# A long convolution with a routed expert layer: the filter stage on single-bank PSUM tensors, with one two-sign copy a bank and products of ones between its groups

## The chip, the cores and the metric

The kernel runs on one core of a Trainium2 chip. The metric is device time in microseconds (us) for one launch. The engines are TensorE (PE; PEld is its weight load), VectorE (DVE), ScalarE (ACT), GpSimd (POOL) and SyncE (SP), which here only issues DMAs.

## What is computed

Inputs `x` and `v` are 4 x 12608 x 128, in float32. A filter is made by a small network over position embeddings, damped by a window, and convolved along the sequence; then 128 rows of each batch pass through an expert layer.

```
h_mlp  = maximum(pos_emb @ w1, 0) @ w2            # 12608x64 @ 64x64, @ 64x128
h_filt = h_mlp * exp(-0.01 * pos)
u = x * v
y = irfft(rfft(u, 2S) * rfft(h_filt, 2S))[:S]     # per batch and channel
x = x * y
scores = x @ w_gate                               # per batch: top 128 rows
x[top] += sigmoid(scores[top]) * (relu(x[top] @ w1e) @ w2e)
```

## The kernel before

The transforms are products with tables of cosines and sines. The sequence is laid out as a 91 x 254 grid. One program does the following in order.

**The filter** runs once, before anything else can finish. It has three stages.

- `h_hid` (L293): position embeddings times `w1`, in eight groups of 16 products (L331; the two halves `h` use different rows of the array). A product in float32 is two passes in the trace, so there are 254 passes for 127 products. A group's output is a two-bank PSUM tensor `c`, three of which rotate. The ReLU with the window goes to `big` (view `hw`) by DVE (L342), or for the second half of odd groups by ACT in eight small instructions (L339). DVE (L346) and POOL (L344) write a second copy with signs. Twenty products of a 128 x 128 bf16 tile of ones (L321) run ahead of the groups.
- `h_spec` (L348), first loop: 256 products of 92 columns (L354, 512 passes), 16 to each of 16 two-bank tensors. ACT alone copies each one to `th` in SBUF (L355), with the frequency outermost in the destination, so that consecutive elements land 512 bytes apart. In this text this loop is the spec loop.
- `h_spec`, second loop: 23 steps `i`. `second(i)` does eight products (L366) into bank `a` number `i % 2`, ACT copies half of it (L369), and DVE forms sum and difference (L372, two instructions). `final(i)` does eight products (L382) into a two-bank tensor: for each half `h` a bank with both signs `s`. ACT copies sign 0 of a bank (L392) and DVE sign 1 (L390) into `big` (view `sp_all`), 364 bytes apart from element to element. `second` runs two steps ahead.

**The main loop** has 128 steps `t` of four channels. `f_s1` (L410) and `dft` (L287) are forward transforms into the banks `a` and into `c1` or `c0` in turn; ACT copies out (L412, L290). DVE combines (`f_v` L419, `f_u` L416), multiplies by the filter (`f_m`, L424 and L425) and adds (`f_y`, L430 and L431). POOL forms `sd` (L437, L438). Three steps later `f_i` (L282) transforms back into `c2`. The first `f_s1` stands ahead of the last `final`. `stage_u` (POOL, L268) multiplies `x` by `v`. The selection of rows and the expert layer run in the gaps of the steps.

The order on each engine is the order in which the code issues. Waits come from tensors: an instruction waits for earlier users of the same PSUM tensor or the same piece of SBUF.

Of the kernel before, what the change touches and what calls it, by code (L numbers as in the profile page):

```python
# [10 lines left out]
F32 = mybir.dt.float32  # L11
AF = mybir.ActivationFunctionType
ALU = mybir.AluOpType
# [5 lines left out]
NQ = 64  # L19
# [160 lines left out]
def hyena_moe(ctx, tc, xg, x2, pos, bw, ww, wg, mw1, mw2, fo, fc, c1, gx, cf, ci, wm, tk, out):  # L180
# [26 lines left out]
    bank2 = [pp.tile([128, 1024], F32, tag=f"c{k}", name=f"c{k}") for k in range(3)]  # L207

    def ps1(k, shape, name):
        return view((*bank1, *bank2[::2])[k], 0, shape)  # L210

    def ps2(k, shape, name):
        return view(bank2[k], 0, shape)
# [70 lines left out]
    def dft(t, te, pq):  # L284
        for w in (1, 0):
            for a in range(0, 128, 32):
                nc.tensor.matmul(pq[w][a:a + 32], lhsT=cf_sb[:, 2 * w + a // NQ, a % NQ:a % NQ + 32],  # L287
                                 rhs=te[:, a // NQ], start=True, stop=True)
        qs = buf("qs", t, [128, HC])
        nc.scalar.copy(out=qs, in_=pq[1])  # L290
        return qs

    def h_hid():  # L293
        pt = view(arena, POS0, [128, PJ, N1])
        wl = view(arena, FILT + 381, [128, FO])
        nc.sync.dma_start(wl, bw)

        def load(k):
            nc.sync.dma_start(pt[:, PC * k:PC * (k + 1)], pos[:, PC * k:PC * (k + 1)])

        for k in range(PJ // PC):
            load(k)
            if k == 1:
                nc.sync.dma_start(wm_sb, wm)
        nc.sync.dma_start(fc_sb, fc)
        nc.sync.dma_start(fo_sb, fo)
        nc.sync.dma_start(ww_sb, ww)
        nc.sync.dma_start(c1_sb, c1)
        nc.sync.dma_start(cf_sb, cf)
        nc.sync.dma_start(ci_sb, ci)  # L310
        nc.sync.dma_start(gx_sb, gx)
        nc.sync.dma_start(wgb, wg.partition_broadcast(128))
        nc.sync.dma_start(tk_sb, tk)
        for k in range(NV):
            load_u(k)
            stage_u(k)

        def warm(n, w):
            wp = ps2(2, [w.shape[0], w.shape[1]], "warm")
            for _ in range(n):  # L320
                nc.tensor.matmul(wp[:w.shape[1]], lhsT=w, rhs=w, start=True, stop=True)  # L321

        warm(20, onesb)
        for k in range(PJ // PC):
            a, z = PC * k, PC * (k + 1)
            ps = ps2(k % 3, [N1, 2, PC, FO], f"hid_{k}")
            for j in range(a, z):
                for h in range(2):
                    if h * PJ + j < N3:
                        r = slice(h * FO, (h + 1) * FO)  # L330
                        nc.tensor.matmul(ps[:, h, j - a], lhsT=pt[r, j], rhs=wl[r], start=True, stop=True)  # L331
            for h in range(2):
                j0, j1 = h * PJ + a, min(h * PJ + z, N3)
                o = hw[:, :, :, j0:j1]
                pv = ps[:, h, :j1 - j0].rearrange("p j d -> p d j")
                wb = wm_sb[:N1, :, j0:j1].unsqueeze(2).to_broadcast([N1, 3, FO, j1 - j0])
                if h and k % 2:
                    for i in range(j1 - j0):
                        nc.scalar.activation(out=o[:, 0, :, i], in_=ps[:, h, i], func=AF.Relu,  # L339
                                             scale=wm_sb[:N1, 0, j0 + i:j0 + i + 1])  # L340
                else:
                    nc.vector.scalar_tensor_tensor(out=o[:, 0], in0=pv, scalar=0.0, in1=wb[:, 0], op0=ALU.max, op1=ALU.mult)  # L342
                if h:
                    nc.gpsimd.tensor_tensor(out=o[:, 1], in0=o[:, 0], in1=wb[:, 1], op=ALU.mult)  # L344
                else:
                    nc.vector.scalar_tensor_tensor(out=o[:, 1], in0=pv, scalar=0.0, in1=wb[:, 2], op0=ALU.max, op1=ALU.mult)  # L346

    def h_spec():  # L348
        for k in range(16):
            e, f = divmod(8 * k, FO)  # L350
            ps = ps2(k % 3, [128, 2, 512], f"ht_{k}")[:, :, :4 * N4].rearrange("p b (f k) -> p b f k", f=4)
            for i in range(8):
                for p in (slice(0, NQ), slice(NQ, N3)):
                    nc.tensor.matmul(ps[p, i // 4, i % 4], lhsT=hw[:, e, f + i, p], rhs=fc_sb, start=True, stop=True)  # L354
            nc.scalar.copy(out=th[:, :, e, f:f + 8].rearrange("p k (b f) -> p b f k", f=4), in_=ps[:N3])  # L355
        for k in range(NV, NU):
            load_u(k)
        stage_u(NV)
        hs = {}

        def second(i):
            ps = ps1(i % 2, [128, 2, 2, 2 * NQ], f"hq_{i}")
            for e in range(2):
                for c in (1, 0):
                    for h in range(2):
                        nc.tensor.matmul(ps[h * FO:(h + 1) * FO, c, e], lhsT=th[:, c * KH + i + KH // 2 * h, e],  # L366
                                         rhs=fo_sb[:N3, e, 1 - c:3 - c].rearrange("p a r -> p (a r)"), start=True, stop=True)
# [3 lines left out]
            for s, op in enumerate((ALU.add, ALU.subtract)):  # L371
                nc.vector.tensor_tensor(out=hs[i][:, s].rearrange("p w e r -> p e w r"),  # L372
                                        in0=ps[:, 0].rearrange("p e (w r) -> p e w r", w=2), in1=sb, op=op)

        def final(i):
            hb = hs.pop(i)
            ps = ps2(i % 3, [128, 2, 2, 2, D], f"hf_{i}")
            for s in range(2):
                for w in range(2):
                    for h in range(2):  # L380
                        r = slice(h * FO, (h + 1) * FO)
                        nc.tensor.matmul(ps[:, h, s, w], lhsT=hb[r, s, w].rearrange("p e r -> p (e r)"), rhs=ww_sb[r],  # L382
                                         start=True, stop=True)
# [12 lines left out]
        second(1)  # L396
        for i in range(n):
            if i == n - 1:
                te[0] = f_s1(0)
            final(i)  # L400
            if i + 2 < n:
                second(i + 2)

    def f_s1(t):
        u = buf("x", t, [NP, 4, N3])
# [660 lines left out]
        else:  # L1066
            picked.append((b, ix, xe))

    for t in bank2[2:] + bank1 + bank2[:2]:
        nc.vector.memset(t, 0.0)  # L1070
    te, uv, ys, sd, ph = {}, {}, {}, {}, {}
    h_hid()
    h_spec()
    ex = None
    bg = Background(iter(()))
    NT = B * NG
    for t in range(NT + LAG):
# [4 lines left out]
        if t < NT:  # L1082
# [4 lines left out]
            qs = dft(t, te.pop(t), (uv[t][:, 0], uv[t][:, 1]))  # L1087
            bg.hook("p", 1)
            bg.hook("n", 1)
            if t + 1 < NT:  # L1090
                te[t + 1] = f_s1(t + 1)
            spare[0] = None
            bg.hook("w", 1)
            load_u(t + NU)
            if t < NG:
                nc.sync.dma_start(hd[:, t], slots[:, t])
            for k in EARLY[t - 4:t - 3] if t > 3 else ():
                nc.scalar.activation(out=view(arena, XP[k], [128, 8 * D]), in_=one.to_broadcast([128, 8 * D]), func=AF.Copy,
                                     scale=0.0)
# [99 lines left out]
```

## Time and profile before

| | |
|---|---|
| median of 3 runs | 873.3 us (871.49 to 873.38) |
| profiled execution | 867.63 us |
| its span in the trace | 865.9 us |
| mean granted TensorE clock | 0.966 of 2.4 GHz |
| PE / PEld busy | 826.7 us (95%) / 697.9 us (81%) |
| DVE / ACT / POOL busy | 706.0 (82%) / 630.2 (73%) / 657.2 us (76%) |

The page cuts the span into 40 slices of 21.6 us and gives each engine's busy share in tenths, and with it the granted clock. The timeline gives instructions in order of start. A row that stands for several (x16) has the time from the first start to the last end, and in brackets how long the engine had been idle and what released it.

### The profile page before, as it was taken

How to read it: one execution, taken by the hardware profiler on the slowest of the kernel's cores; microseconds unless marked ns; L12 is line 12 of the kernel's file. 1: busy time of each engine (PE TensorE's matmuls, PEld its weight loads, DVE VectorE, ACT ScalarE, POOL GpSimd, SP SyncE). 2: the span in 40 equal slices, each digit the busy share in tenths (PEclk: the TensorE clock that was granted, in tenths of full speed). 3: DMA queues.
4: the chain of work that ended last, by engine and by line, in shares of the span. 5: the costliest groups of instructions: out<-in, count | busy, mean ns of one | idle time of the engine just before them, and what ended most of it. 6: DMA issues, size and time to landing. Idle time of an engine off the chain costs nothing.

```text
span 865.9 us, 45183 instructions
## 1 busy us (share of the span) xinstructions
PE 826.7 (95%) x19190; PEld 697.9 (81%) x19190; DVE 706.0 (82%) x1408; ACT 630.2 (73%) x2279; POOL 657.2 (76%) x772
## 2 busy tenths in 40 slices
PE   6999979999999999999999999999999999999975
PEld 6998747777779977777899777788998777779964
DVE  7006769999879889899998898998988989997873
ACT  3555547755556988897659988976599899756971
POOL 0500018999989889899999898998998989989610
PEclk9559999999999999999999999999999999999997
DMA  8000027777887987778879867688798776856910
GB/s 279 31 2 3 2 86 220 216 217 230 260 265 213 332 274 222 211 218 265 257 220 303 305 211 211 213 271 252 223 313 285 220 211 221 261 175 186 317 35 7
DMA packets 77850, 178.41 MB, mean 206 GB/s; under 512 B 9103, under 2 KB 43896, under 8 KB 77648
## 3 DMA queue, kind: packets, MB, share of 16 engines
q1 hardware_dynamic: 73552, 161.23, 59.5%
q10 hardware_dynamic: 3840, 13.76, 4.7%
q8 instruction: 151, 2.47, 1.2%
q0 software_dynamic: 256, 0.52, 0.2%
q14 instruction: 51, 0.42, 0.1%
HBM read 135.77 MB, written 39.71 MB: 203 GB/s over the span
## 4 chain that ended last, share of the span: by engine, by line
PE 83%; DVE 6%; ACT 5%; issue 3%; DMA 2%; SPq 0%; POOL 0%; POOLq 0%; DVEq 0%; ACTq 0%
PE c L282 25%; PE a L410 18%; PE c L287 18%; PE a L526 6%; PE c L530 6%; PE c L354 5%; PE c L526 3%; ACT arena L586 2%; ACT big L392 2%; DVE arena L372 2%; DVE big L390 1%; PE a L530 1%; DMA arena<-in_pos_dram 1%; DMA cf_sb<-in_cf_dram 1%; PE c L278 1%
## 5 line engine op out<-in xcount | busy, mean ns | idle before, releaser
L282 PE MATMUL c<-ci_sb,arena 128*23 128x128 f32 x8128 | 251.6, 273 | 5.1 <-issue 4.7
L282 PEld LDWEIGHTS c<-ci_sb,arena 128*23 128x23 f32 x8128 | 227.7, 103 | 16.3 <-issue 8.6
L437 POOL TENSOR_TENSOR arena<-arena 128x364 f32<-128x364 f32 x127 | 114.1, 898 | 124.4 <-PE c L287 94.7
L287 PE MATMUL c<-arena,cf_sb 128*32 128x364 f32 x2048 | 184.2, 470 | 4.0 <-DVE big L390 2.5
L410 PE MATMUL a<-cons,arena 128*32 128x182 f32 (+1 forms) x4096 | 186.4, 319 | 1.6 <-ACT big L392 1.6
L410 PEld LDWEIGHTS a<-cons,arena 128*32 128x32 f32 (+1 forms) x4096 | 133.3, 110 | 50.3 <-issue 22.8
L586 ACT ACTIVATE arena<-arena 128x128 f32<-128x128 f32 x504 | 148.7, 306 | 10.0 <-DVE arena L576 9.4
L268 POOL TENSOR_TENSOR arena<-arena 128x508 f32<-128x508 f32 x128 | 139.3, 1089 | 19.1 <-DMA arena<-in_xg_dram 19.1
L461 ACT COPY big<-c 128x768 f32<-128x768 f32 x127 | 100.5, 791 | 70.6 <-PE c L282 67.6
L412 ACT COPY arena<-a 128x364 f32<-128x364 f32 x256 | 119.6, 467 | 44.2 <-PE a L410 38.9
L438 POOL TENSOR_TENSOR arena<-arena 128x364 f32<-128x364 f32 x127 | 114.4, 901 | 0.0
L287 PEld LDWEIGHTS c<-arena,cf_sb 128*32 128x32 f32 x2048 | 71.3, 110 | 46.6 <-issue 37.8
L586 ACT ACTIVATION_READ_ACCUMULATOR arena<-arena 128x1 f32 x504 | 99.4, 197 | 0.0
L419 DVE TENSOR_TENSOR c<-c,arena 128x364 f32<-128x364 f32 x128 | 69.7, 544 | 28.0 <-ACT arena L290 26.9
L481 POOL TENSOR_TENSOR big<-big,arena 128x256 f32<-128x256 f32 x128 | 81.7, 638 | 10.0
L424 DVE TENSOR_TENSOR arena<-c,arena 128x728 f32<-128x728 f32 x95 | 86.9, 915 | 2.8
L425 DVE TENSOR_TENSOR c<-c,arena 128x728 f32<-128x728 f32 x95 | 86.9, 915 | 0.0
L480 POOL TENSOR_TENSOR big<-big,arena 128x256 f32<-128x256 f32 x128 | 81.8, 639 | 0.0
L430 DVE TENSOR_TENSOR arena<-c,arena 128x364 f32<-128x364 f32 x127 | 68.3, 538 | 13.1 <-POOL big L480 0.5
L416 DVE TENSOR_TENSOR c<-c,arena 128x364 f32<-128x364 f32 x128 | 69.6, 544 | 2.7
L290 ACT COPY arena<-c 128x364 f32<-128x364 f32 x128 | 59.4, 464 | 16.9 <-PE c L287 7.3
L513 POOL TENSOR_TENSOR arena<-big 128x512 f32<-128x512 f32 x56 | 70.5, 1284 | 0.9 <-PE c L526 0.7
(210 smaller groups left out, 1342.2 us busy)
## 6 DMA issues: line engine op xcount, KB each, us to landing
arena<-in_xg_dram SPq DMA_DIRECT2D x256, 254.0 KB, 3.6
arena<-hd SPq DMA_DIRECT2D x96, 364.0 KB, 4.3
arena<-in_x_dram SPq DMA_DIRECT2D x40, 420.0 KB, 5.4
out_dram<-arena SPq DMA_DIRECT2D x32, 420.0 KB, 5.7
out_dram<-arena ACTq DMA_DIRECT2D x32, 420.0 KB, 5.8
hd<-big SPq DMA_DIRECT2D x32, 364.0 KB, 3.9
arena<-in_x_dram SPq DMA_DIRECT2D x48, 210.0 KB, 4.4
arena<-in_pos_dram SPq DMA_DIRECT2D x8, 364.0 KB, 6.2
```

Source lines behind the costliest of these rows:

```text
L268: nc.gpsimd.tensor_tensor(out=x, in0=x, in1=v, op=ALU.mult)
L282: nc.tensor.matmul(o[32 * k:32 * k + c.stop - c.start], lhsT=lhsT[:, c], rhs=rhs, start=True, stop=True)
L287: nc.tensor.matmul(pq[w][a:a + 32], lhsT=cf_sb[:, 2 * w + a // NQ, a % NQ:a % NQ + 32], rhs=te[:, a // NQ], start=True, stop=True)
L410: nc.tensor.matmul(tps[s // 2][c, s % 2], lhsT=u[:, s, c], rhs=c1_sb[:, k], start=True, stop=True)
L412: nc.scalar.copy(out=te[:, :, 2 * h:2 * h + 2].rearrange("p e s i -> p s e i"), in_=tps[h])
L424: nc.vector.tensor_tensor(out=mt, in0=uv, in1=ht[:, 0].unsqueeze(1).to_broadcast([128, 2, HC]), op=ALU.mult)
L425: nc.vector.tensor_tensor(out=uv, in0=uv, in1=ht[:, 1].unsqueeze(1).to_broadcast([128, 2, HC]), op=ALU.mult)
L437: eng.tensor_tensor(out=nat(sd[:, 0]), in0=nat(yz[:, 0]), in1=rev(yz[:, 1]), op=ALU.add)
L438: eng.tensor_tensor(out=nat(sd[:, 1]), in0=rev(yz[:, 0]), in1=nat(yz[:, 1]), op=ALU.subtract)
L461: nc.scalar.copy(out=ay[:, t % NG, :NJ + JM, ss], in_=o3[:, :, :NJ + JM].rearrange("p s x -> p x s"))
L480: nc.gpsimd.tensor_tensor(out=d, in0=a, in1=stg(t), op=ALU.subtract)
L586: nc.scalar.activation(out=x, in_=x, func=AF.Copy, accum_out=self.sc[:, j:j + 1])
```

## The change

Six edits, all ahead of the main loop's step 1:

1. PSUM in the filter: one two-bank tensor `c1` and four one-bank tensors `f0` to `f3`, which with `a0`, `a1` make six single banks that rotate. The four are given up behind the filter and their place becomes `c0` and `c2`; `c2` is set to zero by ACT at step 0.
2. `h_hid`: each half of a group has a bank of its own; ACT takes the ReLU of the second half in groups 1, 2, 4, 5, 7 (before: 1, 3, 5, 7). Six products of ones follow each group and 28 the last one.
3. Spec loop: 32 tensors of 8 products. ACT and DVE copy them in turn, and the copy now writes four neighbouring elements at a time.
4. `final`: one copy takes both signs of a bank. ACT copies the bank of half 0, DVE that of half 1.
5. The two first `stage_u` move behind the spec loop.
6. `f_s1(0)` stands ahead of `final(21)`; `dft(0)` and `f_s1(1)` stand ahead of `final(22)`.

```diff
-            ps = ps2(k % 3, [N1, 2, PC, FO], f"hid_{k}")
+            ps = [ps1((4, 5, 6, 7, 0, 1)[2 * k % 6 + h], [N1, PC, FO], f"hid_{k}_{h}") for h in range(2)]
...
+            warm(6 if k + 1 < PJ // PC else 28, ps2(1, [128, 128], "warm"))
...
-                if h and k % 2:
+                if h and k in (1, 2, 4, 5, 7):
...
-        for k in range(16):
-            e, f = divmod(8 * k, FO)
-            ps = ps2(k % 3, [128, 2, 512], f"ht_{k}")[:, :, :4 * N4].rearrange("p b (f k) -> p b f k", f=4)
-            for i in range(8):
+        for k in range(32):
+            e, f = divmod(4 * k, FO)
+            ps = ps1((4, 5, 6, 7, 0, 1)[k % 6], [128, 4, N4], f"ht_{k}")
+            for i in range(4):
...
-            nc.scalar.copy(out=th[:, :, e, f:f + 8].rearrange("p k (b f) -> p b f k", f=4), in_=ps[:N3])
+            o, x = th[:, :, e, f:f + 4], ps[:N3].rearrange("p f k -> p k f")
+            if k % 2:
+                nc.vector.tensor_copy(o, x)
+            else:
+                nc.scalar.copy(out=o, in_=x)
+        for k in range(NV):
+            stage_u(k)
...
-            ps = ps2(i % 3, [128, 2, 2, 2, D], f"hf_{i}")
+            ps = [ps1(4 + i % 2 * 2 + h, [128, 2, 2, D], f"hf_{i}_{h}") for h in range(2)]
...
-                for s in range(2 if k else 1):
-                    o = sp_all[:, :, :, :, KH - 1 + (k, -k)[s]].rearrange("p g w s -> p w g s")
-                    x = ps[:, h, s].rearrange("p w (g s) -> p w g s", s=4)
-                    if s:
-                        nc.vector.tensor_copy(o, x)
-                    else:
-                        nc.scalar.copy(out=o, in_=x)
+                ks = slice(KH - 1 - k, KH + k, max(2 * k, 1))
+                o = sp_all[:, :, :, :, ks].rearrange("p g w s k -> p k w g s")
+                x = ps[h][:, :2 if k else 1].rearrange("p k w (g s) -> p k w g s", s=4)
+                if h:
+                    nc.vector.tensor_copy(o, x)
+                else:
+                    nc.scalar.copy(out=o, in_=x)
...
-            if i == n - 1:
+            if i == n - 2:
                 te[0] = f_s1(0)
             final(i)
             if i + 2 < n:
                 second(i + 2)
+            if i == n - 2:
+                pre[0] = dft(0, te.pop(0), ps2(1, [128, 2, 512], "pq_0")[:, :, :HC])
+                te[1] = f_s1(1)
```

DVE in the second loop of the filter, with what each instruction waits for, before (L372 forms sum and difference, L390 copies a sign of `c`):

```order
L390 COPY big<-c_73 128x2x32x4 [waits Activation_49] x2
L372 TENSOR_TENSOR arena<-a_71,arena 128x2x2x64 [waits DVE_49,Activation_49]
L372 TENSOR_TENSOR arena<-a_71,arena 128x2x2x64 [waits DVE_49]
L390 COPY big<-c_74 128x2x32x4 [waits Activation_49] x2
L372 TENSOR_TENSOR arena<-a_70,arena 128x2x2x64 [waits DVE_49,Activation_49]
L372 TENSOR_TENSOR arena<-a_70,arena 128x2x2x64 [waits DVE_49]
```

And now (L380 is sum and difference, L398 the copy of a bank):

```order
L398 COPY big<-f_79 128x2x2x32x4 [waits PE_49]
L380 TENSOR_TENSOR arena<-a_71,arena 128x2x2x64 [waits Activation_49]
L380 TENSOR_TENSOR arena<-a_71,arena 128x2x2x64 [waits DVE_49]
L398 COPY big<-f_77 128x2x2x32x4 [waits PE_49]
L380 TENSOR_TENSOR arena<-a_70,arena 128x2x2x64 [waits Activation_49]
L380 TENSOR_TENSOR arena<-a_70,arena 128x2x2x64 [waits DVE_49]
```

Two copies a step that each waited for ACT have become one of twice the size that waits for PE alone.

PE from the last `second` to the main loop's second `dft`, before (L382 is `final`, L410 `f_s1`, L287 `dft`):

```order
L366 MATMUL a_70<-arena 64x128 x8
L382 MATMUL c_72<-arena 128x128 x8
L410 MATMUL a_70<-cons,arena 32x182 x3
...
L410 MATMUL a_71<-cons,arena 31x182
L382 MATMUL c_73<-arena 128x128 x8
L287 MATMUL c_73<-arena,cf_sb 32x364 x8
L410 MATMUL a_70<-cons,arena 32x182 x3
...
L287 MATMUL c_72<-arena,cf_sb 32x364 x8
```

And now (L390 is `final`, whose two banks alternate; L421 `f_s1`, L290 `dft`):

```order
L374 MATMUL a_70<-arena 64x128 x8
L421 MATMUL a_70<-cons,arena 32x182 x3
...
L390 MATMUL f_78<-arena 128x128
...
L290 MATMUL c_72<-arena,cf_sb 32x364 x8
L421 MATMUL a_70<-cons,arena 32x182 x3
...
L390 MATMUL f_76<-arena 128x128
...
L290 MATMUL c_1234<-arena,cf_sb 32x364 x8
```

`f_s1(0)` is now followed by two `final`, and `dft(0)` and `f_s1(1)` stand between these.

## Rows read from the trace of the kernel before

**Rows 1.** The page, part 2: PE busy and granted clock in 40 slices.

```profile
PE   6999979999999999999999999999999999999975
PEclk9559999999999999999999999999999999999997
```

**Rows 2.** Windows of 2 us, PE alone: length, busy (passes), granted clock, DMA, GB/s.

```profile
4.00:6.00 2.00, 1.77 (x27) 1.00 0.96 322
6.00:8.00 2.00, 1.92 (x48) 1.00 1.00 368
62.00:64.00 2.00, 1.92 (x22) 0.60 0.00 0
122.00:124.00 2.00, 2.00 (x28) 0.50 0.23 92
```

**Rows 3.** Windows by stage: length, then PE, PEld, DVE, ACT, POOL, and the clock.

```profile
4.75:17.50 12.75, 11.55 (x254) 11.02 (x254) 10.93 (x19) 4.61 (x22) 0.00 (x0) 1.00 0.95 334
21.08:60.00 38.92, 38.92 (x508) 38.92 (x510) 0.00 (x0) 21.65 (x15) 12.93 (x11) 0.50 0.07 21
```

**Rows 4.** Timeline, PE and ACT around the first stage: start, length, idle before and its releaser.

```profile
2.22 2.29 PE L321 MATMUL c<-onesb 128*128 128x128 bf16 x20 [2.22 <-DVE c L1070]
...
19.45 1.57 ACT L339 ACTIVATE big<-c,arena 91x64 f32<-91x64 f32 x7 [1.21 <-DVE big L346]
...
21.08 9.16 PE L354 MATMUL c<-arena,big 91*63 91x92 f32 x116 [1.89 <-ACT big L339]
```

**Rows 5.** Groups by line, first 132 us: count, busy, mean ns of one, idle before.

```profile
L392 ACT COPY big<-c 128x256 f32<-128x256 f32 x46 | 27.6, 604 | 24.2 <-DVE big L390 22.1 <-PE c L382 2.0
L390 DVE COPY big<-c 128x256 f32<-128x256 f32 x45 | 26.9, 599 | 17.6 <-ACT big L392 17.6
L355 ACT COPY arena<-c 127x736 f32<-127x736 f32 x16 | 23.0, 1440 | 18.0 <-PE c L354 18.0
L369 ACT COPY arena<-a 128x256 f32<-128x256 f32 x23 | 9.4, 409 | 2.0 <-PE a L366 2.0
```

**Rows 6.** The page, part 5: the main loop's copy that writes four neighbours at a time.

```profile
L461 ACT COPY big<-c 128x768 f32<-128x768 f32 x127 | 100.5, 791 | 70.6 <-PE c L282 67.6
```

**Rows 7.** Timeline where the spec loop ends.

```profile
60.63 1.39 ACT L355 COPY arena<-c 127x736 f32<-127x736 f32 x1 [1.04 <-PE c L354]
62.08 2.26 PE L366 MATMUL a<-arena 127*64 127x128 f32 x24 [0.63 <-ACT arena L355]
```

**Rows 8.** Timeline of the second loop: steps 0, 1 and 20 of `final`, and one step's copies.

```profile
64.27 1.16 PE L382 MATMUL c<-arena 64*128 64x128 f32 x16
66.39 1.16 PE L382 MATMUL c<-arena 64*128 64x128 f32 x16
...
76.58 0.61 DVE L390 COPY big<-c 128x256 f32<-128x256 f32 x1 [0.66 <-ACT big L392]
77.03 0.74 DVE L372 TENSOR_TENSOR arena<-a,arena 128x256 f32<-128x256 f32 x2
78.31 0.59 ACT L392 COPY big<-c 128x256 f32<-128x256 f32 x1 [1.04 <-DVE big L390]
...
110.54 1.16 PE L382 MATMUL c<-arena 64*128 64x128 f32 x16 [0.16 <-DVE arena L372]
```

**Rows 9.** Timeline from the filter's end into the main loop.

```profile
115.65 1.44 PE L410 MATMUL a<-cons,arena 128*32 128x182 f32 x32 [1.59 <-ACT big L392]
...
120.73 1.82 PE L287 MATMUL c<-arena,cf_sb 128*32 128x364 f32 x16 [2.55 <-DVE big L390]
...
123.09 0.55 DVE L419 TENSOR_TENSOR c<-c,arena 128x364 f32<-128x364 f32 x1 [2.42 <-ACT arena L290]
...
126.49 0.52 DVE L431 TENSOR_TENSOR arena<-arena,c 128x364 f32<-128x364 f32 x1
...
128.90 1.43 PE L287 MATMUL c<-arena,cf_sb 128*32 128x364 f32 x16 [0.64 <-ACT arena L412]
...
130.15 1.42 PE L410 MATMUL a<-cons,arena 128*32 128x182 f32 x32
131.38 1.93 PE L282 MATMUL c<-ci_sb,arena 128*23 128x128 f32 x64
135.58 1.93 PE L282 MATMUL c<-ci_sb,arena 128*23 128x128 f32 x64
```

More of the change, by code (lines that the diff above doesn't have):

```diff
@@ L206, in hyena_moe @@
     bank1 = [pp.tile([128, 512], F32, tag=f"a{k}", name=f"a{k}") for k in range(2)]
-    bank2 = [pp.tile([128, 1024], F32, tag=f"c{k}", name=f"c{k}") for k in range(3)]
+    bank2 = [None, pp.tile([128, 1024], F32, tag="c1", name="c1"), None]
+    fs = ExitStack()
+    fp = fs.enter_context(tc.tile_pool(name="fp", bufs=1, space=PSUM))
+    ring = [fp.tile([128, 512], F32, tag=f"f{k}", name=f"f{k}") for k in range(4)]
     def ps1(k, shape, name):
-        return view((*bank1, *bank2[::2])[k], 0, shape)
+        return view((*bank1, *bank2[::2], *ring)[k], 0, shape)
     def ps2(k, shape, name):
@@ L286, in dft @@
             for a in range(0, 128, 32):
-                nc.tensor.matmul(pq[w][a:a + 32], lhsT=cf_sb[:, 2 * w + a // NQ, a % NQ:a % NQ + 32],
+                nc.tensor.matmul(pq[a:a + 32, w], lhsT=cf_sb[:, 2 * w + a // NQ, a % NQ:a % NQ + 32],
                                  rhs=te[:, a // NQ], start=True, stop=True)
         qs = buf("qs", t, [128, HC])
-        nc.scalar.copy(out=qs, in_=pq[1])
+        nc.scalar.copy(out=qs, in_=pq[:, 1])
         return qs
@@ L315, in h_hid, with warm @@
             load_u(k)
-            stage_u(k)
-        def warm(n, w):
-            wp = ps2(2, [w.shape[0], w.shape[1]], "warm")
+        def warm(n, wp):
             for _ in range(n):
-                nc.tensor.matmul(wp[:w.shape[1]], lhsT=w, rhs=w, start=True, stop=True)
-        warm(20, onesb)
+                nc.tensor.matmul(wp, lhsT=onesb, rhs=onesb, start=True, stop=True)
+        warm(20, ps2(1, [128, 128], "warm"))
         for k in range(PJ // PC):
             a, z = PC * k, PC * (k + 1)
-            ps = ps2(k % 3, [N1, 2, PC, FO], f"hid_{k}")
+            ps = [ps1((4, 5, 6, 7, 0, 1)[2 * k % 6 + h], [N1, PC, FO], f"hid_{k}_{h}") for h in range(2)]
             for j in range(a, z):
@@ L330, in h_hid @@
                         r = slice(h * FO, (h + 1) * FO)
-                        nc.tensor.matmul(ps[:, h, j - a], lhsT=pt[r, j], rhs=wl[r], start=True, stop=True)
+                        nc.tensor.matmul(ps[h][:, j - a], lhsT=pt[r, j], rhs=wl[r], start=True, stop=True)
+            warm(6 if k + 1 < PJ // PC else 28, ps2(1, [128, 128], "warm"))
             for h in range(2):
@@ L370, in second @@
             hs[i] = view(arena, HS0 + 768 + i % 3 * 512, [128, 2, 2, 2, NQ])
-            for s, op in enumerate((ALU.add, ALU.subtract)):
+            for s, op in enumerate((ALU.subtract, ALU.add)):
                 nc.vector.tensor_tensor(out=hs[i][:, s].rearrange("p w e r -> p e w r"),
@@ L381, in final @@
                         r = slice(h * FO, (h + 1) * FO)
-                        nc.tensor.matmul(ps[:, h, s, w], lhsT=hb[r, s, w].rearrange("p e r -> p (e r)"), rhs=ww_sb[r],
+                        nc.tensor.matmul(ps[h][:, s, w], lhsT=hb[r, s, w].rearrange("p e r -> p (e r)"), rhs=ww_sb[r],
                                          start=True, stop=True)
@@ L1067, in topk_one @@
             picked.append((b, ix, xe))
-    for t in bank2[2:] + bank1 + bank2[:2]:
+    for t in bank2[1:2] + ring + bank1:
         nc.vector.memset(t, 0.0)
-    te, uv, ys, sd, ph = {}, {}, {}, {}, {}
+    te, uv, ys, sd, ph, pre = {}, {}, {}, {}, {}, {}
     h_hid()
     h_spec()
+    fs.close()
+    ring.clear()
+    qp = ctx.enter_context(tc.tile_pool(name="qp", bufs=1, space=PSUM))
+    for k in (0, 2):
+        bank2[k] = qp.tile([128, 1024], F32, tag=f"c{k}", name=f"c{k}")
     ex = None
@@ L1086, in hyena_moe @@
             bg.now = t
-            qs = dft(t, te.pop(t), (uv[t][:, 0], uv[t][:, 1]))
+            qs = pre.pop(t) if t in pre else dft(t, te.pop(t), uv[t])
             bg.hook("p", 1)
             bg.hook("n", 1)
-            if t + 1 < NT:
+            if t + 1 < NT and t + 1 not in te:
                 te[t + 1] = f_s1(t + 1)
@@ L1096, in hyena_moe @@
                 nc.sync.dma_start(hd[:, t], slots[:, t])
+            if t == 0:
+                nc.scalar.activation(out=bank2[2], in_=one.to_broadcast([128, 1024]), func=AF.Copy, scale=0.0)
             for k in EARLY[t - 4:t - 3] if t > 3 else ():
```

6 lines of the change are left out of this document (3 added, 3 removed).

## The prediction

> **What bounds the kernel now.** I read the slices first. PE is 90% busy or more in nearly every slice, and the granted clock is near full in all but two: the second and third slice, 21.6 to 65 us, read 5 [rows 1]. So PE bounds the main loop, and there is a stretch ahead of it in which PE is busy at half speed. What the change is worth is decided there, because all six edits lie ahead of step 1 of the main loop, and what PE does from the first `f_i` on (131.38 us, a step every 4.2 us with no idle time printed [rows 9]) stays the same work in the same order. A microsecond saved ahead of that row is a microsecond saved in the end.
>
> Next the windows by stage. In the first stage PE is busy 11.55 of 12.75 us, 254 passes at 45.5 ns, clock 1.00. In the spec loop it has no idle time at all: 508 passes in 38.92 us, 76.6 ns each, clock 0.50, with DVE at zero and ACT 56% busy [rows 3]. So neither the copies nor a transfer bounds the spec loop. PE does, at 1.2 GHz. The clock reaches 1.00 only at about 63 us, when `second` has begun: the window 62 to 64 reads 0.60 [rows 2]. It had been lost where PE stood idle at the end of the first stage, for DVE and then for the last small ReLUs on ACT (ending at 21.02 us; PE released after 1.89 us of idle) [rows 4].
>
> Here a page differs from a row. The 39 us of gapless products of the spec loop did not raise the clock [rows 3]. The Trainium skill, page "TensorE: Matmul & The Clock Gate", section "Part 1: The HAM clock gate (the "warmup" mystery)", says that half rate is the default and that sustained matmul activity releases it. By that alone the spec loop would have mended itself and the clock term below would be worth nothing. The measurement decides: not every busy stream raises the clock, so it matters at which clock the stage is entered.
>
> Last, the second loop. Its first steps are 2.12 us apart (64.27 to 66.39). Over the 20 steps to 110.54 the mean is 2.31, because ACT and DVE take turns: the DVE copy of a sign idles 0.66 us for ACT's, ACT's idles 1.04 for DVE's [rows 8], and over all steps DVE idles 17.6 us and ACT 22.1 on one another [rows 5].
>
> **The change part by part.** Times are on the profiled execution (867.63 us, span 865.9).
>
> *First stage.* Eight groups of 32 passes at 45.5 ns are 11.65 us. The 42 ones between groups come on top, since they stand in PE's order. Their price at full clock is in no row. The 20 at the start took 2.29 us, 114 ns each, and the clock reads 1.00 [rows 4]; but real passes in 4 to 6 us took 65 ns and those in 6 to 8 us 40 [rows 2], so I read those first microseconds as half clock and take 57 ns for the later ones. The ends of the bound are 57 and 114. So 42 are 2.4 us, and the last group ends at 4.75 + 11.65 + 2.4 = 18.8. ACT's last seven ReLUs need 1.57 behind it (20.4), and the 28 ones last until 20.4 as well, so PE has almost no idle time there. The spec loop starts at 20.5 instead of 21.08: **0.6 saved**. POOL's eight sign products now start with the groups, with `stage_u` out of their way; they are needed only in the second half of the spec loop.
>
> *Spec loop.* At full clock 512 passes cost half of 76.6, 38.3 ns: 19.6 instead of 39.2 us, **19.6 saved**. The upper end is 45.5 ns a pass, as in the first stage (3.7 us less). Do the copies keep up? A tensor of 8 products takes PE 0.61 us, so each engine has 1.23 us for one copy of 368 elements. By the old copy's rate (1440 ns for 736 scattered elements [rows 5]) it would be about 0.75; by ACT's copy in fours (791 ns for 768 [rows 6]) under 0.5. Either fits; six banks give slack. Behind the last copy, 1.39 us long, the passes of `second` go on (62.08 [rows 7]); the copy of half the size takes some 0.55: **0.85 saved**. From there to the first `final` (64.27 [rows 8]) it was 2.19 us, with 24 passes that took 2.26 mostly at half clock [rows 7]. At full clock I take 1.5 for these and the first sum on DVE, an estimate between half of 2.26 and 2.19: **0.7 saved**.
>
> *Second loop.* DVE waits for PE alone now. Its copy of 512 elements lies between 0.60, the price of 256, and twice that; old and new copies scatter alike, so I take the upper end, 1.2 [rows 5]. With 0.74 for sum and difference [rows 8] that is 1.94 us a step, under PE's 2.12. ACT: the slope from 256 to 736 scattered elements gives 1.05 for 512, plus 0.41 (L369) [rows 5]. So PE paces, 20 steps of 2.12 = 42.4 instead of 46.27 us (64.27 to 110.54 [rows 8]): **3.9 saved**.
>
> *Into the main loop.* Before, 20.84 us lie between `final(20)` and the first `f_i` (131.38), among them PE idle of 1.59 and 2.55 us [rows 9]. Now, from the start of `final(20)`: `f_s1(0)` needs the banks `a`, that is ACT's copy of a bank (from 1.26 to 2.3), L369 (2.7), sum and difference (3.5). Everything behind it on PE waits too, so some 1.3 us of idle stay. Then `f_s1` 1.23, `final(21)` 1.1, `dft(0)` 1.25, `f_s1(1)` 1.23, `final(22)` 1.1 end at 9.5. Its copies last until 10.75; `dft(1)` waits for them, because its bank is one of theirs, and so does `f_v(0)` on DVE. From `f_v(0)` DVE needs 3.9 us to the end of `f_y(0)` (123.09 to 127.01 [rows 9]), which frees `c1`; `dft(2)` and `f_s1(3)` take 2.5, and `f_i(0)` starts at 17.2: **3.6 saved**. ACT's zeroing of `c2` lies in the 6.5 us before it. The clock had dropped behind the 2.55 us of idle, to 0.50 [rows 2]; a drop now would cost about 1 us, which I keep for the range.
>
> Sum: 0.6 + 19.6 + 0.85 + 0.7 + 3.9 + 3.6 = 29.25 us, 838.4 for the profiled execution. The median of the runs shown is 5.7 above that execution, so I forecast 873.3 - 29.25 = **844.0**.
>
> **The rivals.**
>
> *A, the forecast.* The spec loop is entered and kept at full clock. For it: the first stage's products at full clock, with gaps, held 1.00 from 4.75 to 17.5 [rows 3]; those of the spec loop at full clock leave smaller gaps. With the unknowns at their far ends: ones at 114 ns (4.0), passes at 45.5 (3.7), a drop at the end (1) give 853; a spec loop that starts with DVE's end (about 19.4), no wait ahead of `f_s1(0)` (1.3) and the runs' own spread (1.8) give 840, 838 with a step of 2.0.
>
> *B, the ones do not do their work.* The clock falls soon after the spec loop has begun, because its products do not count for enough: they left it at 0.50 for 39 us [rows 3]. Then 19.6 and 0.7 are not gained: 864. The Trainium skill's page "TensorE: Matmul & The Clock Gate", section "A second HAM failure mode: psum-queue depth-cycling", speaks for this: cycling through PSUM banks leaves small idles at which the clock went up and down, and the change cycles through twice as many small tensors. The trace bears that out little: the first stage cycled through three tensors at 1.00 [rows 3].
>
> *C, the copies pace the second loop.* If 512 scattered elements cost more than twice 256, or the two engines hinder each other, a step stays at the mean of 2.31 and the 3.9 are not gained: 848; at 2.5 a step it would be 852. Against it: both ran side by side before at their usual 0.6 [rows 8].
>
> *D, slower.* The ones hold up the first stage and the clock falls there already. 254 passes at 91 instead of 45.5 ns cost 11.6, 70 ones at 114 cost 4 more than counted, and the spec loop gains nothing (20.3): 880. It decides from about 60% of the first stage at half clock. Against it, rows 3 again: the same passes held 1.00 without any ones between.
>
> **How the numbers follow.** A 0.76, B 0.13, C 0.08, D 0.03. The likeliest is A: 844. A's own range is 838 to 853 and C lies inside it; B and D with A's tails are the 2 in 10 outside. About 0.2% (1.7 us) is what a measurement of this kernel can tell from no change; A, B and C are faster by more, D is slower, and 0.01 I keep for B with some further loss: faster 0.96, same 0.01, slower 0.03.
>
> **What would show it.** Right: clock 9 in the second and third slice, 512 passes of the spec loop in about 20 us, steps of `final` 2.1 us apart, no DVE copy released by ACT, the first `f_i` near 102 us, and behind it 4.2 us a step as before. Wrong: clock 0.50 inside the spec loop (B), PE in the second loop released by DVE (C), the spec loop starting after 24 us (ones dearer than counted, or D), or a main loop whose steps have grown.

## The result, and the profile after

The changed kernel took 847.26 us (median of four launches: 836.59, 841.12, 853.41, 855.06), the kernel before beside it 872.39 us (four launches, 871.22 to 873.38). The ratio is 0.9616, with a 95% interval of 0.9564 to 0.9668; in the ratios given here, launches over 1.5% above the shortest of their kernel are left out, while the medians hold all launches. By medians it is 0.9712. The forecast was 844.0 with a range of 838 to 853. The median lies in that range, but no launch lay near 844 or 847: there are two of about 839 and two of about 854. Most of the experiments went into that.

The profiled execution took 841.12 us, span 839.3, against 867.63 and 865.9 before. Parts 1 and 2 of its page (busy us, share and count for each engine; PE's busy share and the granted clock in 40 slices):

```profile
PE 809.7 (96%) x19260; PEld 702.4 (84%) x19260; DVE 714.5 (85%) x1403; ACT 618.0 (74%) x2265; POOL 656.5 (78%) x772
PE   8999899999999999999999999999999999999975
PEclk9999999999999999999999999999999999999997
```

The two slices that read 5 [rows 1] read 9. PE is busy 17 us less than before, although 70 products of ones were added: the products of the spec loop now run at 2.4 instead of 1.2 GHz.

PE in the filter, after (timeline: start, length, instruction, count, idle time before and its releaser):

```profile
2.22 2.29 PE L322 MATMUL c<-onesb 128*128 128x128 bf16 x20 [2.22 <-DVE c L1081]
4.57 2.23 PE L332 MATMUL f<-arena 64*91 64x64 f32 x32
6.73 0.51 PE L322 MATMUL c<-onesb 128*128 128x128 bf16 x6
7.17 1.51 PE L332 MATMUL f<-arena 64*91 64x64 f32 x32
...
18.45 1.50 PE L332 MATMUL f<-arena 64*91 64x64 f32 x30
19.89 1.74 PE L322 MATMUL c<-onesb 128*128 128x128 bf16 x28
21.55 2.75 PE L356 MATMUL f<-arena,big 91*64 91x92 f32 x64
...
40.61 1.43 PE L356 MATMUL f<-arena,big 91*64 91x92 f32 x32
41.87 0.61 PE L374 MATMUL a<-arena 127*64 127x128 f32 x8
42.78 1.53 PE L374 MATMUL a<-arena 127*64 127x128 f32 x24 [0.30 <-DVE arena L359]
44.36 1.16 PE L390 MATMUL f<-arena 64*128 64x128 f32 x16
...
86.71 1.16 PE L390 MATMUL f<-arena 64*128 64x128 f32 x16
```

From the first group to the end of the spec loop no idle time is printed: where PE idled 1.89 us before [rows 4], and 1.29 us shortly ahead of that, 28 ones run. The spec loop takes 20.32 us (21.55 to 41.87; 512 passes at 39.7 ns, before 76.6 [rows 3]). The last line is step 20 of `final`: 42.35 us for 20 steps, 2.12 each.

The copies of these loops by line, first 105 us (count, then busy us, mean ns of one, and idle time with its releaser; the spec loop's other copies go from bank `a`, with the same means):

```profile
L398 DVE COPY big<-f 128x512 f32<-128x512 f32 x23 | 23.8, 1033 | 5.7 <-PE f L390 5.5
L400 ACT COPY big<-f 128x512 f32<-128x512 f32 (+1 forms) x23 | 23.4, 1018 | 15.2 <-PE f L390 15.2
L359 DVE COPY arena<-f 127x368 f32<-127x368 f32 x11 | 6.0, 541 | 9.1 <-PE f L356 9.1
L361 ACT COPY arena<-f 127x368 f32<-127x368 f32 x11 | 5.1, 465 | 9.1 <-PE f L356 9.1
```

Hardly any copy waits for the other engine any more; in [rows 5] DVE and ACT idled 17.6 and 22.1 us on one another. A bank of 512 scattered elements costs 1.03 us, 1.7 times the 0.60 of 256. The spec copy takes 0.47 and 0.54 us for 368 elements in fours; the old one took 1.44 for 736 apart.

Into the main loop, after (timeline):

```profile
90.41 1.44 PE L421 MATMUL a<-cons,arena 128*32 128x182 f32 x32 [1.51 <-DVE arena L380]
...
97.57 0.58 DVE L430 TENSOR_TENSOR c<-c,arena 128x364 f32<-128x364 f32 x1
...
97.87 1.43 PE L290 MATMUL c<-arena,cf_sb 128*32 128x364 f32 x16 [1.24 <-DVE big L398]
...
101.07 0.52 DVE L442 TENSOR_TENSOR arena<-arena,c 128x364 f32<-128x364 f32 x1
...
101.74 1.43 PE L290 MATMUL c<-arena,cf_sb 128*32 128x364 f32 x16 [1.21 <-DVE arena L442]
...
104.20 1.96 PE L285 MATMUL c<-ci_sb,arena 128*23 128x128 f32 x64
```

The three waits are those the prediction named: `f_s1(0)` for sum and difference, `dft(1)` for the last `final`'s copies, `dft(2)` for `f_y(0)`. The first `f_i` starts at 104.20 instead of 131.38 [rows 9], 27.18 us earlier. The time behind it is 735.10 us (839.3 - 104.20), before 734.52: 0.6 us of the gain is given back there.

### The profile page after: what moved, and what is told of

Read it like the earlier page. It is cut to its first block, busy times and chain, and to the rows that moved or that the text cites. A ratio compares the mean times of both kernels' runs of the same rounds, so it can differ in the third digit from the quotient of the medians.

```text
span 839.3 us, 45295 instructions
## 1 busy us (share of the span) xinstructions
PE 809.7 (96%) x19260; PEld 702.4 (84%) x19260; DVE 714.5 (85%) x1403; ACT 618.0 (74%) x2265; POOL 656.5 (78%) x772
## 4 chain that ended last, share of the span: by engine, by line
PE 84%; DVE 9%; ACT 3%; issue 2%; DMA 1%; POOL 1%; POOLq 0%; DVEq 0%; ACTq 0%
PE c L285 25%; PE a L421 18%; PE c L290 18%; PE a L537 6%; PE c L541 6%; PE c L537 3%; DVE big L398 2%; DVE arena L380 2%; PE f L356 2%; ACT arena L597 2%; PE f L332 1%; PE a L541 1%; ACT arena L377 1%; PE c L322 1%; PE a L356 1%
## 5 line engine op out<-in xcount | busy, mean ns | idle before, releaser
L285 PEld LDWEIGHTS c<-ci_sb,arena 128*23 128x23 f32 x8128 | 232.3, 103 | 11.4 <-issue 6.9
L290 PE MATMUL c<-arena,cf_sb 128*32 128x364 f32 x2048 | 186.4, 469 | 3.5 <-DVE big L398 1.2
L421 PE MATMUL a<-cons,arena 128*32 128x182 f32 (+1 forms) x4096 | 187.9, 318 | 1.5 <-DVE arena L380 1.5
L421 PEld LDWEIGHTS a<-cons,arena 128*32 128x32 f32 (+1 forms) x4096 | 146.2, 110 | 36.5 <-issue 10.4
L290 PEld LDWEIGHTS c<-arena,cf_sb 128*32 128x32 f32 x2048 | 76.2, 110 | 43.0 <-issue 21.2
L597 ACT ACTIVATION_READ_ACCUMULATOR arena<-arena 128x1 f32 x504 | 94.5, 188 | 0.0
```

What stands on the lines that cost most here:

```text
L285: nc.tensor.matmul(o[32 * k:32 * k + c.stop - c.start], lhsT=lhsT[:, c], rhs=rhs, start=True, stop=True)
L290: nc.tensor.matmul(pq[a:a + 32, w], lhsT=cf_sb[:, 2 * w + a // NQ, a % NQ:a % NQ + 32], rhs=te[:, a // NQ], start=True, stop=True)
L421: nc.tensor.matmul(tps[s // 2][c, s % 2], lhsT=u[:, s, c], rhs=c1_sb[:, k], start=True, stop=True)
L597: nc.scalar.activation(out=x, in_=x, func=AF.Copy, accum_out=self.sc[:, j:j + 1])
```

## The experiments

All keep the whole computation. Where a time has no edit beside it, it is a launch or the median of launches of that kernel. In the expectations T1 is the prediction's reason on the point in question and T2 its rival; K1 is the theory that came out of the first four: the two kinds of launches differ in whether the clock is up during the first stage.

**e1, the changed kernel once more.** No edit, another chip.

> The changed kernel once more, unchanged, since its four runs spread from 837 to 855 us while those of the kernel before lie within 2.2. Theory M1: the spread lies in the main loop, with the filter alike in every run: the first f_i starts at 104 +- 0.5 us, and what follows it takes 731 us in a short run and up to 749 in a long one. Theory M2: the spread lies in the filter, where the clock rises at a different moment or falls for part of the spec loop: then the first f_i moves by up to 14 us and what follows takes 735 us always.

Measured: 840.08, 840.88, 853.38, 854.74, 855.16 and 855.42 us, median 854.06; the kernel before on that chip 870.26, median of 11 launches from 850.66 to 876.15; ratio 0.985 (0.978 to 0.992). The profiled launch (840.88) repeats the trace above, first `f_i` at 104.08. It is a short one, so it does not decide between M1 and M2. The two groups of times belong to the kernel: with the first four, four launches in ten at 837 to 841, six at 853 to 855, none between. And the kernel before spreads over 25 us on this chip, which its first four launches had not shown. So the 3.8% of the first comparison, short launches of the one kernel against launches of 871 us and more of the other, is not what the change is worth everywhere: here it is 1.5%.

**e2, without the 42 and the 28 ones.**

```diff
-            warm(6 if k + 1 < PJ // PC else 28, ps2(1, [128, 128], "warm"))
```

> The changed kernel without the 42 products of ones between the groups and the 28 behind the last (the 20 at the start stay). Theory T1: the ones hold the clock. PE idles for DVE's and ACT's last ReLUs at the end of the first stage, the clock falls to 0.50 there, and the spec loop's 512 passes take 39 us at 76.6 ns; the first stage is some 2.5 us shorter. First f_i near 104.2 + 19.6 + 0.7 - 2.5 = 122 us, time 16 to 19 us above the changed kernel. Theory T2: the single banks and the fifth group on ACT shorten the wait at the end of the first stage so far that the clock stays without the ones: spec loop at 1.00, first f_i near 101.5 us, time 2 to 3 us below the changed kernel.

Measured: 838.22, 853.88, 862.25 and 863.82 us, median 858.07. The trace is of the shortest launch. PE's timeline where its spec loop begins:

```profile
18.02 2.94 PE L355 MATMUL f<-arena,big 91*64 91x92 f32 x63 [1.28 <-DVE big L343]
```

Here PE idled 1.28 us and the clock stayed at 1.00 all the same; the spec loop began 3.5 us earlier and the first `f_i` came at 100.92. In this launch the ones were a pure cost. The three others lie 16 to 26 us above it, and the trace of one launch could not say why. e9 took this up: the mean granted clock recorded for the launch of 853.88 is 0.972, as in both launches of e9.

**e3, the ones alone, in the kernel before.** The ones go to bank `a0`.

```diff
...
+            warm(6 if k + 1 < PJ // PC else 28, ps1(0, [128, 128], "warm"))
```

> The kernel before with the same 42 and 28 products of ones added (into bank a0) and nothing else. Theory T1: the spec loop is entered at 1.00 and keeps it; now ACT's sixteen scattered copies of 1.44 us pace it, not PE's 1.23: 16 x 1.5 = 24 us instead of 39.2. First f_i near 131.4 - 15 - 0.7 + 1 = 117 us, time 14 us below the kernel before. Theory T2: small idles behind the copies let the clock fall again inside the spec loop, as products that could not raise it cannot hold it: spec loop 35 to 39 us, first f_i 128 to 132 us.

Measured: 850.8, 860.83, 863.04 and 869.37 us, median 861.93, against 870.26 for the kernel before on that chip; the ratio is 1.006 (0.995 to 1.017), so by the times alone a gain of the ones is not shown. The trace is of the longest. PE from the last ones on:

```profile
33.99 21.10 PE L354 MATMUL c<-arena,big 91*64 91x92 f32 x512
...
57.17 1.53 PE L366 MATMUL a<-arena 127*64 127x128 f32 x24 [1.64 <-ACT arena L355]
...
67.27 1.16 PE L382 MATMUL c<-arena 64*128 64x128 f32 x16
...
69.63 1.16 PE L382 MATMUL c<-arena 64*128 64x128 f32 x16 [0.18 <-DVE arena L372]
```

The trace's clock record has the rise at 35.28 us, and the old spec loop, too, runs at full clock from there (21.10 us for 512 passes). ACT's single chain of copies now lags (1.64 us of idle ahead of `second`), and the steps of `final` still grow from 2.12 to 2.36 (mean of 20: 2.31, as before). But the loop starts at 33.99: in this launch the whole first stage ran at half clock. So there is a second place where the clock decides, about 12 us in size, and the ones behind the groups do not touch it.

**e4, the changed kernel with the old copies**, one sign each, from the new single banks.

```diff
-                ks = slice(KH - 1 - k, KH + k, max(2 * k, 1))
...
+                for s in range(2 if k else 1):
+                    o = sp_all[:, :, :, :, KH - 1 + (-k, k)[s]].rearrange("p g w s -> p w g s")
+                    x = ps[h][:, s].rearrange("p w (g s) -> p w g s", s=4)
...
```

> The changed kernel with the old copies in final: ACT copies one sign of each bank and DVE the other, four copies of 256 elements a step instead of two of 512. Theory T1: two engines on one bank wait for each other again; a step of final goes from 2.12 to 2.31 or 2.36 us, 23 steps 4.4 to 5.5 us longer; first f_i near 109 us. Theory T2: it was the third two-bank tensor and not the sharing that set the step; steps stay at 2.12 and the first f_i at 104 us.

Measured: 839.13, 851.51, 857.66 and 858.1 us, median 854.59. The second loop of the launch of 851.51 (groups by line, then PE's timeline):

```profile
L400 ACT COPY big<-f 128x256 f32<-128x256 f32 x46 | 23.8, 618 | 15.2 <-PE f L390 15.2
L398 DVE COPY big<-f 128x256 f32<-128x256 f32 x45 | 23.6, 597 | 16.9 <-ACT big L400 16.9
```

```profile
70.00 1.16 PE L390 MATMUL f<-arena 64*128 64x128 f32 x16
...
72.11 1.16 PE L390 MATMUL f<-arena 64*128 64x128 f32 x16
```

T1 falls here. DVE still waits for ACT, 16.9 us in all against 17.6 before the change, and yet the step is 2.12 with no idle time on PE. What has gone is the wait in the other direction: ACT waits for PE alone. So the shorter step comes from the single-bank tensors, in which ACT's next bank is not held by DVE's copy of the last one; the two-sign copy is worth nothing to the step.

The same trace has its first stage at half clock, PE's timeline again:

```profile
4.54 2.71 PE L332 MATMUL f<-arena 64*91 64x64 f32 x32
7.19 0.82 PE L322 MATMUL c<-onesb 128*128 128x128 bf16 x6
...
30.98 3.17 PE L322 MATMUL c<-onesb 128*128 128x128 bf16 x28
34.08 3.16 PE L356 MATMUL f<-arena,big 91*64 91x92 f32 x64
```

A group of 32 passes takes 2.65 us instead of 1.44, six ones 0.75 instead of 0.44. The 42 ones between the groups do not raise the clock in 26 us. Behind the 28 it goes up: the trace's clock record has the rise at 34.95 us, 0.87 us into the spec loop, whose passes go from 75 to 40 ns. The spec loop starts 12.5 us later than in the trace of the changed kernel, the first `f_i` 13.7 later, and 841.12 + 13.7 is 854.8: the long launches. This launch itself took 851.51, because what lies behind the first `f_i` took 731.8 us in it; over the eleven traces of this study that stretch takes 730.7 to 741.9 us. No long launch of the changed kernel itself is in a trace. What is on record of them fits a start at half clock and not a fall in the main loop: their mean granted clock, 0.992 to 0.994, is that of the short ones, and 12.5 us lost by a fall would take 25 us at half clock, 0.015 off the mean (an estimate from the two levels). A half-clock start does not lower it, since the record reads 1.00 until its first change (last section).

**e5, no ones at the start.**

```diff
-        warm(20, ps2(1, [128, 128], "warm"))
```

> The changed kernel without the 20 products of ones at the start (the 42 and the 28 stay). In the trace of the kernel with the old sign copies the clock stayed at half until 34.95 us, when the 28 ones had run, and the whole filter ended 13 us later than in the short runs. Theory K1: this is what tells long runs from short ones; the 20 ones at the start raise the clock at about 6 us in some launches and miss in others. Without them every run is a long one, 853 to 857 us, the clock rises near 35 us and the first f_i starts near 117.5 us. Theory K2: the spread has another cause and the 20 ones don't matter: the runs still spread from 840 to 855, and in a short one the clock rises by 12 us and the first f_i is at 104 us.

Measured: ten launches from 851.79 to 859.06 us, median 855.98. Not one is short. The kernel before on that chip has a median of 861.26 us, 18 launches from 848.36 to 876.19; the ratio is 1.001 (0.997 to 1.005), so with this start the changed kernel cannot be told from the shorter launches of the kernel before. Around the spec loop's start, PE:

```profile
30.92 3.17 PE L322 MATMUL c<-onesb 128*128 128x128 bf16 x28
34.01 2.82 PE L355 MATMUL f<-arena,big 91*64 91x92 f32 x64
```

The first stage is again at half clock to its end, the clock rises at 34.20 us, behind the 28 ones, and the first `f_i` starts at 116.73.

**e6, forty ones at the start.**

```diff
-        warm(20, ps2(1, [128, 128], "warm"))
+        warm(40, ps2(1, [128, 128], "warm"))
```

> The changed kernel with 40 instead of 20 products of ones at the start; they end near 6.6 instead of 4.5 us, so the first group starts 2 us later. Theory K1: whatever the moment of the launch, the clock rises by 7 to 9 us, so every run is short: 841 to 844 us, spread under 3 us, first f_i at 105 to 106.5 us. Theory K2: the spread does not hang on the start: runs from 841 to 857 us as before.

Measured on the chip of e5: 841.7, 842.08, 842.24, 842.76, 843.24, 843.38 and 849.31 us, median 842.76; ratio to the kernel before 0.986 (0.981 to 0.991). PE's first stage:

```profile
2.22 4.42 PE L322 MATMUL c<-onesb 128*128 128x128 bf16 x40 [2.22 <-DVE c L1081]
6.58 1.70 PE L332 MATMUL f<-arena 64*91 64x64 f32 x32
...
19.93 1.50 PE L332 MATMUL f<-arena 64*91 64x64 f32 x30
```

The clock rises at 7.01 us. With 20 more ones, 2 us, the long launches are gone. K1 holds: none of the ten launches without starting ones is short, four in ten with 20 (on two other chips; the kernel with 20 was not launched on this one), and all seven with 40 stay under 850. The one of 849.31 was the profiled one; its first `f_i` starts at 105.67, and the main loop behind it took 6.7 us longer than the changed kernel's (741.8 against 735.1). A fall of the clock at 232 us lasts 3.4 us and explains at most 1.7 of them; the rest has another cause, not looked into.

**e7, what e2, e4, e5 and e6 suggest, in one kernel.** Forty ones from 1.10 us on (the bank is zeroed behind them instead of ahead), none between the groups, 20 behind the last; `f_s1(0)` behind `final(21)`; `dft(0)` and `f_s1(1)` behind `final(22)`.

```diff
-        warm(20, ps2(1, [128, 128], "warm"))
+        warm(40, ps2(1, [128, 128], "warm"))
+        nc.vector.memset(bank2[1], 0.0)
...
-            warm(6 if k + 1 < PJ // PC else 28, ps2(1, [128, 128], "warm"))
+            if k + 1 == PJ // PC:
+                warm(20, ps2(1, [128, 128], "warm"))
...
-            if i == n - 2:
-                te[0] = f_s1(0)
             final(i)
...
             if i == n - 2:
+                te[0] = f_s1(0)
+            if i == n - 1:
...
-    for t in bank2[1:2] + ring + bank1:
+    for t in ring + bank1:
```

> What the earlier runs point to, in one version: 40 ones at the start that begin about 1 us earlier (c1 is set to zero behind them and not ahead), no ones between the groups and 20 behind the last, f_s1(0) behind final(21) and dft(0) and f_s1(1) behind final(22). Theory K1: the clock is raised in every launch and the ones between groups only lengthen PE's first stage (44 ns x 10 a group): spec loop from about 18.5 us instead of 21.55, and from final(20) to the first f_i 14.5 instead of 17.5 us: first f_i near 98 us, every run 833 to 837 us. Rival: without the 42 ones the clock falls again at the end of the first stage in some launches, and runs of 850 us and more remain; or the seam is bound by DVE's chain and not by the copies of final(22), and it stays at 17.5 us.

Measured, again on the chip of e5: 835.23 to 841.74 us, median 838.36 of six; ratio to the kernel before 0.981 (0.976 to 0.987). PE's timeline:

```profile
1.10 3.68 PE L322 MATMUL c<-onesb 128*128 128x128 bf16 x40 [1.10 <-DVE onesb L245]
...
17.60 2.75 PE L358 MATMUL f<-arena,big 91*64 91x92 f32 x64 [0.36 <-DVE big L346]
...
86.46 1.44 PE L423 MATMUL a<-cons,arena 128*32 128x182 f32 x32 [0.42 <-DVE arena L382]
...
98.01 1.93 PE L285 MATMUL c<-ci_sb,arena 128*23 128x128 f32 x64
```

The clock rises at 3.80 us and stays up through the spec loop, with no ones between the groups and 20 behind the last. The spec loop starts 3.95 us earlier than after the change. From the start of `final(20)` (82.76) to the first `f_i` it is 15.25 us instead of 17.49: `f_s1(0)` waits 0.42 instead of 1.51 us, as a `final` now fills that wait. Of the 6.2 us by which the first `f_i` is earlier, 3.4 reach the end of the span. On that chip this kernel is 4.4 us under the one with 40 ones and has no long launch; it is the best of this study.

**e8, the kernel before, in the trace once more.** No edit.

> The kernel before, unchanged, on another chip: its times reached from 848 to 876 us there, so the question is what its short launches have. If the clock decides them (theory K1: whether the first stage ends with the clock up), a launch under 860 us shows the spec loop's 512 passes at about 40 ns (20.5 us instead of 41.0) and the first f_i at 108 to 112 us instead of 131.38, with the same 734.5 us behind it; a launch of 867 or more shows the spec loop at 76.6 ns or a first stage at twice its time. If the main loop decides them (rival), the first f_i stands near 131 in a short launch too, and what follows is shorter than 734.5 by the difference.

Measured: one launch, 866.62 us, like the first. PE at the spec loop's start, and windows (length, PE busy and passes, granted clock, DMA share, GB/s):

```profile
19.02 0.37 PE L354 MATMUL c<-arena,big 91*64 91x92 f32 x2 [1.30 <-DVE big L342]
21.29 5.02 PE L354 MATMUL c<-arena,big 91*63 91x92 f32 x62 [1.89 <-ACT big L339]
```

```profile
16.00:20.00 4.00, 2.10 (x44) 0.98 0.91 317
20.00:24.00 4.00, 2.71 (x36) 0.50 0.30 87
30.00:40.00 10.00, 10.00 (x134) 0.50 0.01 2
```

It repeats [rows 3] and [rows 4] on another chip: PE idles 1.30 us, runs two passes, idles 1.89 us, and the spec loop then runs at 0.50. The clock falls at 19.84 us, within the second idle (in the first trace at 19.23). What its launches of 848 to 858 us have was not caught in a trace and stays open. The recorded clock speaks for K1: on the chips of e1 and e5 the launches under 856 us have means of 0.982 to 0.988, those of 867 to 869 us 0.963 to 0.966. That is some 30 us less at half clock, about the 16 us by which they are shorter (an estimate: a microsecond at half clock does half the work). Those of 870 to 876 us read 0.988 to 0.992, which fits a half-clock start as in e3 and e4; neither is shown by a trace.

**e9, forty ones at the start and none behind the groups.** The run that asks what the 28 ones do, with the start taken out of the question.

```diff
-        warm(20, ps2(1, [128, 128], "warm"))
+        warm(40, ps2(1, [128, 128], "warm"))
...
-            warm(6 if k + 1 < PJ // PC else 28, ps2(1, [128, 128], "warm"))
```

> The changed kernel with 40 ones at the start instead of 20, and without the 42 ones between the groups and the 28 behind the last. If the ones in the layer's gaps do nothing once the clock is up (theory T2), this is the run with 40 at the start less 3.5 us (first f_i near 102.2 instead of 105.67): 838 to 841 us in nearly every launch, clock 1.00 through the spec loop. If the 28 ones are what brings the clock to the spec loop where the first stage's end leaves PE idle (theory T1, the prediction's), launches fall to half clock in the spec loop as the kernel before did: 858 to 862 us in a good part of the launches, with 0.50 in the windows from 20 to 60 us when one is profiled.

Measured, on the chip of e8: 852.27 and 856.69 us, somewhat under T1's 858 to 862. PE's first stage and the spec loop's start, and windows of PE:

```profile
6.58 3.14 PE L332 MATMUL f<-arena 64*91 64x64 f32 x64
...
14.73 2.75 PE L332 MATMUL f<-arena 64*91 64x64 f32 x62
...
19.36 2.93 PE L355 MATMUL f<-arena,big 91*64 91x92 f32 x54 [1.89 <-DVE big L343]
```

```profile
10.00:16.00 6.00, 6.00 (x154) 1.00 0.89 297
20.00:24.00 4.00, 4.00 (x70) 0.62 0.24 63
30.00:40.00 10.00, 10.00 (x134) 0.50 0.01 2
50.00:60.00 10.00, 9.95 (x132) 0.57 0.01 2
```

T1 holds. The first stage holds 1.00 without ones between its groups, and from its first group to the end of its last it takes 10.9 us where e6, with the 42 ones, takes 14.85. Then PE idles 1.89 us. The spec loop begins at 1.00 and the clock falls at 20.98 us, 1.6 us into it; the 512 passes take 37.8 us (19.36 to 57.20). The first `f_i` starts at 119.73, 14 us behind the run with 40 ones at the start and the others kept, although 70 ones fewer were run. Of the two groups of ones that were taken out, those behind the last group are what carries the clock into the spec loop: e7, which has only these, keeps it. It also held without them in the one launch above in which the idle was 1.28 us.

## Why the prediction was right

By its own steps, on the profiled executions:

| term | predicted, us | measured, us |
|---|---|---|
| first stage (start of the spec loop) | 0.6 saved | 0.5 lost (21.08 to 21.55) |
| spec loop and its last copy | 20.45 saved | 19.8 (41.00 to 21.23) |
| start of the first `final` | 0.7 saved | 0.6 (2.19 to 1.58) |
| second loop, 20 steps | 3.9 saved | 3.9 (46.27 to 42.35) |
| into the main loop | 3.6 saved | 3.35 (20.84 to 17.49) |
| behind the first `f_i` | 0 | 0.6 lost |
| sum | 29.25 | 26.6 |

- **Spec loop.** Right in size and in cause. Where PE idles at the end of the first stage the clock is lost: within the idle in the kernel before (1.29 and 1.89 us with two passes between), 1.6 us behind it in e9 (1.89 us). The 28 ones fill that place, and the loop then stays at 2.4 GHz. Its copies kept up. Rival B did not occur: in no trace did the clock fall in a spec loop that followed on the ones. What B describes, a clock that falls soon after the loop has begun, is what e9 shows without the ones. Cycling through six single banks cost no clock: in the trace of the changed kernel it stays at 1.00 from 6.14 us to the end of the filter and on. The Trainium skill, page "TensorE: Matmul & The Clock Gate", section "A second HAM failure mode: psum-queue depth-cycling", tells of another kernel whose clock went up and down as it cycled through banks. The trace shows nothing of that kind here.
- **First stage.** The sign was wrong. In the rows six ones take 0.44 us, 73 ns each instead of 57, and the first group ran mostly at half clock (2.16 instead of 1.44 us), which had been left out. The 42 cost more than their own rows show, since a group takes 1.44 us with ones around it and 1.30 without (e9): the first stage is 3.95 us shorter without them (14.85 in e6, 10.9 in e9), 94 ns for each. Only the 28 in a row, 59 ns each, were priced right.
- **Second loop.** Right in size, wrong in the reason. The prediction gave it to the two-sign copy, with which DVE waits for PE alone; e4 shows that the split into single banks is enough. Its price for the copy, 1.2 us, was too high on DVE (1.03) and near on ACT (1.05 against 1.02). Rival C did not occur.
- **Into the main loop.** Right, wait for wait; `f_i` came 17.49 us behind `final(20)` instead of 17.2.
- **Behind the first `f_i`.** "A microsecond saved ahead of that row is a microsecond saved in the end" holds for the two traces of the table to 0.6 us. In general it holds only within the 11 us by which this stretch differs from trace to trace.
- **The median.** The sum came close: 838.4 for an execution like the profiled one, 841.12 measured. That the median, too, came near 844.0 is luck. It is the middle of two kinds of launches, 847.26 being the mean of 841.12 and 853.41, and that there are two was not foreseen. Nor was a cause given for the 5.7 us that were added because the median before lay that far above the traced execution. By the recorded clocks (e8) launches of over 870 us are probably such as start at half clock, which the traced one did not.
- **Rival D.** One step failed, the argument against D, "the same passes held 1.00 without any ones between". It is true of the launch in the trace from 5.58 us on, where its clock record begins with a rise, and of e9, once the clock is up; it says nothing of a launch in which the 20 ones at the start leave it down. Half of D came true in six of ten launches, by their times and the trace of e4: a first stage at half clock, 12.5 us. The cause is the start, not that the ones hold up the stage. The other half did not, since the clock comes back behind the 28 ones, within 1.3 us of the spec loop's start (e3, e4, e5). Without that they would, by estimate, have kept next to nothing: 854.8 and the 17.5 us by which the spec loop of e9 is longer (37.84 against 20.32) make 872.3, the time before.

Of the change's edits, then, the 28 ones, the single banks and the new places of `f_s1` and `dft` earn what is gained, the last by the traces alone. The 42 ones between the groups earn nothing: at full clock they cost 3.95 us, and at half clock they do not raise it.

## What to carry to other kernels

Look at the time of one pass at both ends of a stage, and fill an idle stretch of PE ahead of a long run of products rather than the gaps inside a stage that already holds its clock. One trace shows one launch: where the clock has to rise at the start, see how the times of many launches group, and give the start enough products that all of them begin alike. Two engines that empty one PSUM tensor wait for each other in this code; a tensor for each bank ends the wait that set the step, without any change to the copies.

## What was not expected of the hardware

- Which products ran ahead of a rise. Gapless float32 products, 91 rows by 92 columns, left the clock at 1.2 GHz for 39 us twice (the kernel before) and 36 us once (e9, 20.98 to 57.20); first-stage groups with six ones between them left it there for 26 us (e3, e4, e5). Twenty-eight bf16 products of 128 x 128, 3.1 us long, were each time followed by a rise (34.20 to 35.28 us in e3, e4 and e5). It is not a matter of float32 as such: behind the spec loop at half clock the rise came 0.5 to 3.5 us after the float32 products of `second` (127 rows by 128 columns) had begun (60.80 us in e8, 58.52 in e9, 63.60 in the first trace).
- The same 20 ones at the start raise the clock at about 6 us in some launches (5.58 to 6.43 us in five traces: two of each kernel, and e2) and not at all in others (e3, e4). The Trainium skill, page "TensorE: Matmul & The Clock Gate", section "Part 1: The HAM clock gate (the "warmup" mystery)", says that the number of slow products at a start differs from run to run of one kernel. The runs agree, and here such a difference lasted not a few products but the whole first stage: 12.5 us.
- The clock column of the profile reads 1.00 until the first change is recorded, even where passes take 83 ns: e4's page reads 9 in its first slices although the stage ran at half clock. At a program's start the time of a pass is the better witness.
- Copies that write single elements far apart cost about 2 ns an element (1.02 and 1.03 us for 512), those that write four neighbours 1.3 to 1.5 (0.465 and 0.541 us for 368).
